# Causal scores as 64x64 tiles in a linear-attention and expert kernel, with their evacuation split over two engines

## The chip, the cores and the metric

The kernel runs on one core of one Trainium2 chip. The metric is the device time of one execution in microseconds (us). A core has a matrix engine (TensorE, PE; its weight loads are shown as PEld), VectorE (DVE), ScalarE (ACT), GpSimd (POOL) and SyncE (SP), which issues most transfers. Each engine works through its own instructions in order; semaphores order the engines among each other.

## The reference, cut to what matters

Two parts follow each other. The first is a linear attention with a decay for each channel; the second a router that sends each token to two of eight experts.

```python
# q, k, v, f_logit: (B, H, S, D) = (4, 8, 768, 48), float32
f = 1.0 / (1.0 + np.exp(-f_logit))
for t in range(S):
    state = f[:, :, t, :, None] * state + np.einsum('bhd,bhe->bhde', k[:, :, t], v[:, :, t])
    y[:, :, t] = np.einsum('bhd,bhde->bhe', q[:, :, t], state)
x = y.transpose(0, 2, 1, 3).reshape(B * S, H * D)            # (3072, 384)
noisy = x @ w_gate + np.log1p(np.exp(x @ w_noise)) * noise    # (3072, 8)
# the two largest of each row, softmax over them; for expert e of its tokens:
out[mask] += weight * (np.maximum(x[mask] @ w1[e], 0) @ w2[e])   # w1 384x1024, w2 1024x384
```

## The kernel before

**Attention.** The sequence is cut into 6 chunks of C = 128 tokens; with 4 batches this gives 24 blocks, n = 0 to 23, chunk n // 4 of batch n % 4. The 8 heads lie in 4 pairs (hp); the two heads of a pair (par) take 64 partitions each, 48 channels padded to 64. For one block the stages are:

- `forget(n)`: PE turns f over (fp, L533), ACT takes exp and ln (L538, L539) and copies the first column to a cap (L542).
- `summed(n)`: DVE's scan along the tokens gives the summed log decay L (L547).
- `decays(n)`: ACT makes P = exp(-L) and Q = exp(L) (L552, L554) and keeps the last column (far, L555).
- `scaled(n)`: PE turns q and k over (qp, kp, L533); DVE multiplies them out of PSUM by P and Q: qP (L559), kQ (L561).
- `scores(n)`: PE turns kQ back (kp, L567; ACT copies it to kn, L569), then eight products of 64 rows by 128 columns give the scores sc of 128 keys by 128 queries for each head (L573), into two banks of PSUM; DVE multiplies all of it by the causal mask into A (L576).
- `output(n)`: y is the sum of two products in two banks: v with A (L591), and from the second chunk on the state with qP (L602); between them the state's growth ds (L597). ACT copies both halves of y (yT, L606) and ds (dss, L611); POOL makes the new state.
- `features(n)`: PE puts y into token rows and gives the router's logits (xp, L626); DVE sums the logits (lg, L629), ACT copies the rows (xs, L631), SP stores them.

**Order.** The order of the program is the order of tracing, fixed on every engine at the end. Step i of the loop traces, one after the other, `forget(i+3)`, `scaled(i+1)`, `scores(i)`, `summed(i+2)`, `output(i-1)`, `decays(i+2)`, `features(i-2)`. After each stage comes a piece of the router of a finished chunk, among them three small ACT functions (sp, L646 to L648), one more (ex, L663), small DVE operations, and two small products on PE (rk, L690, L691). The single-bank tiles of PSUM (`one_bank`) come from six buffers; a new tile waits for the last reader of the buffer that has come free. The tile sc has a pool of its own with two banks.

**Head.** SP loads the first blocks. DVE writes `ones` and the padding; warming products of `ones` with itself (L1233) keep PE busy, six at first and four after each of the steps i = -3, -2 and -1. `clamp(n)` bounds f from below, on DVE for blocks 0 and 1, on POOL after that (L527). Between clamp 3 and clamp 4 POOL writes the fixed part of the router's table w_rt (L1241, L1244) and `carry` (L1246, L1247); the rest of w_rt comes by eight small transfers from POOL's queue (L496).

**Experts.** From about 150 us on PE runs the products of the eight experts (L907, L932, L1014), with gathers and scattered additions through POOL's queue. The first pieces of it stand among the last attention steps.

Of the kernel before, what the change touches and what calls it, by code (L numbers as in the profile page):

```python
# [10 lines left out]
F32 = mybir.dt.float32  # L11
# [5 lines left out]
ALU = mybir.AluOpType  # L17
# [314 lines left out]
def kernel(  # L332
# [38 lines left out]
    nc = tc.nc  # L371
    B, H, S, D = q.shape
# [3 lines left out]
    C = 128  # L376
    NCH = S // C
    HP = H // 2
    DP = 64
# [37 lines left out]
    wk = attention.enter_context(tc.tile_pool(name="wk", bufs=2))  # L417
    ps2 = attention.enter_context(tc.tile_pool(name="ps2", bufs=1, space=PSUM))
    turns = [ps1]

    def one_bank(name):
        turns.append(turns.pop(0))
        return turns[-1].tile([128, 512], F32, tag="one", name=name)

    def two_banks(name):
        return ps2.tile([128, 2, 512], F32, tag="two", name=name)


    ident = const.tile([128, 128], F32, tag="ident", name="ident")
# [36 lines left out]
    causal = const.tile([128, 128], F32, tag="causal", name="causal")  # L466
# [20 lines left out]
    w_rt = const.tile([128, HP, XW + 2 * E], F32, tag="w_rt", name="w_rt")  # L487
# [14 lines left out]
    carry = const.tile([128, E, B + 1], F32, tag="carry", name="carry")  # L502
    upto = [None] * NCH
    far = const.tile([128, NCH * B, HP], F32, tag="far", name="far")
    state = [None] * B
# [6 lines left out]
    def rows(par):  # L512
        return slice(par * DP, (par + 1) * DP)

    def cols(hp):
        return slice(hp * C, (hp + 1) * C)
# [46 lines left out]
    def scores(n):  # L563
        if n // B < NCH - 1:
            kp = one_bank(f"kp_{n}")
            for hp in range(HP):
                nc.tensor.transpose(kp[:, cols(hp)], kQ[n][:, cols(hp)], ident)  # L567
            kn[n] = wk.tile([C, H, DP], F32, tag="kn", name=f"kn_{n}")
            nc.scalar.copy(kn[n].rearrange("t h d -> t (h d)"), kp)  # L569
        sc = two_banks(f"sc_{n}")  # L570
        for hp in range(HP):
            for par in range(2):
                nc.tensor.matmul(sc[:, par, cols(hp)], lhsT=kQ[n][rows(par), cols(hp)],  # L573
                                 rhs=qP[n][rows(par), cols(hp)], start=True, stop=True)
        A[n] = wk.tile([C, 2, HP * C], F32, tag="A", name=f"A_{n}")
        nc.vector.tensor_tensor(A[n].rearrange("j r (a i) -> j (r a) i", i=C), sc.rearrange("j r (a i) -> j (r a) i", i=C),  # L576
                                causal.unsqueeze(1).broadcast_to((C, H, C)), ALU.mult)

    def output(n):
        c, b = n // B, n % B  # L580
        vt = pads["v"][n % RING["v"]]


        y = [one_bank(f"y{odd}_{n}") for odd in range(2)]

        def at(hp, par):
            return y[hp % 2][rows(par ^ hp % 2), cols(hp // 2)]

        for hp in range(HP):
            for par in range(2):  # L590
                nc.tensor.matmul(at(hp, par), lhsT=vt[:, 2 * hp + par, :], rhs=A[n][:, par, cols(hp)],  # L591
                                 start=(hp < 2), stop=(c == 0 and hp >= HP - 2))
        if c < NCH - 1:
            ds = one_bank(f"ds_{n}")
            for hp in range(HP):
                for par in range(2):
                    nc.tensor.matmul(ds[rows(par), hp * DP:(hp + 1) * DP], lhsT=kn[n][:, 2 * hp + par, :],  # L597
                                     rhs=vt[:, 2 * hp + par, :], start=True, stop=True)
        if c:
            for hp in range(HP):  # L600
                for par in range(2):
                    nc.tensor.matmul(at(hp, par), lhsT=state[b][rows(par), hp, :],  # L602
                                     rhs=qP[n][rows(par), cols(hp)], start=False, stop=(hp >= HP - 2))
        yT[n] = wk.tile([128, 2, HP // 2 * C], F32, tag="yT", name=f"yT_{n}")
        for odd in range(2):
            nc.scalar.copy(yT[n][:, odd, :], y[odd][:, 0:HP // 2 * C])  # L606
        if c == NCH - 1:
            return

        dsv = wk.tile([128, HP, DP], F32, tag="ds", name=f"dss_{n}")  # L610
        nc.scalar.copy(dsv, ds[:, 0:HP * DP].rearrange("d (a e) -> d a e", e=DP))  # L611
        end = P[n].rearrange("d (a t) -> d a t", t=C)[:, :, C - 1:C].broadcast_to((128, HP, DP))
        new = wk.tile([128, HP, DP], F32, tag=f"st{b}", name=f"st_{n}")
        if c == 0:
            nc.gpsimd.tensor_tensor(new, dsv, end, ALU.mult)
        else:
            mid = wk.tile([128, HP, DP], F32, tag="mid", name=f"mid_{n}")
            nc.gpsimd.tensor_tensor(mid, dsv, state[b], ALU.add)
            nc.gpsimd.tensor_tensor(new, mid, end, ALU.mult)
        state[b] = new  # L620
# [617 lines left out]
    pad("v")  # L1238
    clamp(2)
    clamp(3)  # L1240
    nc.gpsimd.memset(w_rt, 0.0)  # L1241
    for odd in range(2):
        for r in range(2):
            nc.gpsimd.tensor_copy(w_rt[:, odd::2, r * D:(r + 1) * D],  # L1244
                                  ident[:, (r ^ odd) * DP:(r ^ odd) * DP + D].unsqueeze(1).broadcast_to((128, HP // 2, D)))
    nc.gpsimd.memset(carry, 1.0)  # L1246
    nc.gpsimd.memset(carry[:, :, 0:1], 0.0)  # L1247

    def zeros(count):
        for _ in range(count):  # L1250
# [7 lines left out]
    def first_loads():  # L1258
# [4 lines left out]
        for what, p, pause in (("fetch", 1, 4), ("first", 0, 0), ("second", 0, 3), ("fetch", 2, 5), ("first", 1, 1), ("second", 1, 6),  # L1263
# [13 lines left out]
            for _ in range(pause):  # L1277
                yield

    def tables():  # L1280
        for i, val in enumerate((0, 0, FAR, 0)):
            nc.gpsimd.memset(empty[:, :, i], val)
        nc.gpsimd.memset(entry, 0)
        for i, ids in ((0, row_of), (2, token)):
            nc.gpsimd.tensor_copy(entry[:, :, :, :, i], ids.unsqueeze(3).broadcast_to((128, NCH, B, 2)))
        nc.gpsimd.memset(zero, 0.0)
# [5 lines left out]
    for i in range(-3, NS + 2):  # L1292
        order = [(forget, -3), (scaled, -1), (scores, 0), (summed, -2), (output, 1), (decays, -2), (features, 2)]
        if i < 0:
            order[0:2] = order[1::-1]
        for stage, lag in order:
            n = i - lag
            if not 0 <= n < NS:
                continue
            stage(n)  # L1300
            if stage is forget:
                load("f", n + 4)
                if n > 1:
                    clamp(n + 2)
                if n == 5:
                    tables()
            elif stage is scaled:
                for nm in "qk":
                    load(nm, n + 2) if n < 4 else load(nm, n + 3)
                    if n == 3:  # L1310
                        load(nm, n + 3)
                if n in (1, 2):
                    load_router(n - 1)
            elif stage is scores:
                for m in (n + 1,) if n < 4 else (2 * n - 3, 2 * n - 2) if n < 6 else (n + 3,):
                    load("v", m)
                if n in (2, 6, 7, 8, 9, 10):
                    load_router(2 + (2, 6, 7, 8, 9, 10).index(n))
                elif n == 5:
                    nc.sync.dma_start(out=lists.rearrange("(p r) w -> p r w", p=128), in_=empty)  # L1320
            elif stage is output:
                while xw:
                    xw.pop(0)()
                if 9 <= n < 17:
                    part_of_weights(0, 1 + (n - 9) // 4, (n - 9) % 4)
                elif n >= NS - 2:
                    part_of_weights(1, 1, 1 + (n - NS + 2) * 2)
            elif stage is features and n >= NS - 4:
                part_of_weights(1, 1, (n - NS + 4) * 2) if n < NS - 2 else zeros(4)
            next(router, None)  # L1330
            slot += 1
            if puts and slot % (2 if n_routed == HALF else 3) == 0 and not (done["fetch"] and not done["gather"]):
                puts.pop(0)()
            next(first_pairs, None)

            if done["turned"] and (n_first < 5 or i >= NS - 3 and stage is not forget) and (n_first < 11 or i >= NS - 1):
                next(pieces)
                n_first += 1
        if i < 0:
            warm_up(4)  # L1340
        if i >= NS - 1:
            while xw:
                xw.pop(0)()
        n = i - 2
        if n >= 0 and n % B == B - 1:
            c = n // B
            router = chain(router, route(c))
            n_routed = c + 1
            if c == HALF - 1:
                router = chain(router, enough())  # L1350
                first_pairs = first_loads()
            if c == NCH - 1:
                router = chain(router, plan(), beyond())
# [79 lines left out]
```

## Time and profile before

| what | value |
|---|---|
| median of 3 runs | 652.21 us (651.7 to 653.2) |
| the profiled execution | 652.09 us, span 650.3 us |
| PE busy | 634.9 us, 98% of the span |
| DVE, POOL, ACT busy | 443.4, 270.4, 253.9 us |
| attention steps with a state product, xp to xp | 6.00 us (88.71 to 94.71), 6.4 to 6.6 where the router's product falls in |
| scores sc (L573), 16 passes | 1.09 us of PE in a step |
| first fp on PE | 4.03 us |
| last xp on PE | 151.83 us |

The span runs from the first to the last instruction of the program. In the lines of the profile "x16" counts instructions, and each float32 product that isn't a transposition shows as two. In a timeline line the first number is the start, the second the time from the first start to the last end, and in brackets stands the idle time just before it and what ended it.

### The profile page before, as it was taken

The numbers are of one execution on the slowest core, as the hardware profiler recorded it, in microseconds if no ns is written. First come the engines' busy times: TensorE is split into PE (matmuls) and PEld (weight loads), VectorE is DVE, ScalarE is ACT, GpSimd is POOL, SyncE is SP. The second block draws the span as 40 slices with busy tenths as digits, with TensorE's granted clock in tenths as the row PEclk, the third lists the DMA queues.
The fourth block names the chain that finished last, engine by engine and source line by source line (L and its number), as shares of the span: only waits on it lengthen the run. The fifth ranks groups of instructions, "written<-read, shape, count | busy, mean of one in ns | idle before, by whom it ended". The sixth has DMA issues, their size and how long they took to land.

```text
span 650.3 us, 12900 instructions
## 1 busy us (share of the span) xinstructions
PE 634.9 (98%) x4883; PEld 549.6 (85%) x4883; DVE 443.4 (68%) x993; ACT 253.9 (39%) x602; POOL 270.4 (42%) x301
## 2 busy tenths in 40 slices
PE   8999999999999999999999999999999999999991
PEld 8999999989999999989659956985797589899891
DVE  6777878875766477776757666666666566867851
ACT  6976776752222233343333233223323322333320
POOL 7733999863474540532603350343145014413021
PEclk9999999999999999999999999999999999999997
DMA  9999888969896332459609361844376057502112
GB/s 186 194 229 209 182 192 173 205 173 341 256 214 172 74 74 98 96 135 308 195 1 305 46 191 40 281 99 120 105 217 156 33 178 168 172 3 30 17 26 29
DMA packets 153896, 96.30 MB, mean 148 GB/s; under 512 B 115600, under 2 KB 146320, under 8 KB 153824
## 3 DMA queue, kind: packets, MB, share of 16 engines
q1 hardware_dynamic: 141648, 76.12, 42.6%
q0 software_dynamic: 12176, 19.25, 15.1%
q8 instruction: 41, 0.67, 0.4%
q14 instruction: 31, 0.25, 0.1%
HBM read 75.97 MB, written 19.62 MB: 147 GB/s over the span
## 4 chain that ended last, share of the span: by engine, by line
PE 95%; POOL 1%; DMA 1%; SPq 0%; DVE 0%; issue 0%; POOLq 0%
PE y L1014 33%; PE P L932 8%; PE hp L907 6%; PE W L932 5%; PE Z L932 5%; PE V L932 5%; PE X L932 5%; PE xp L626 4%; PE sc L573 4%; PE y L591 4%; PE xgp L855 2%; PE y L602 2%; PE kp L533 2%; PE qp L533 1%; PE ds L597 1%; PE fp L533 1%
## 5 line engine op out<-in xcount | busy, mean ns | idle before, releaser
L1023 POOL DMA_INDIRECT out_dram<-ys,slots x48 | 80.8, 1683 | 162.2 <-ACT ys L1084 132.9
L1014 PE MATMUL y<-qk_all,f_all 128*128 128x192 f32 x576 | 105.3, 327 | 0.0
L1014 PEld LDWEIGHTS y<-qk_all,f_all 128*128 128x128 f32 x576 | 93.3, 190 | 0.4 <-DVE f_all L996 0.4
L819 POOL DMA_INDIRECT xg<-x_rows,slots x48 | 52.6, 1095 | 30.8 <-DMA slots<-lists 15.5
L703 POOL DMA_INDIRECT lists<-entry,sloti x48 | 54.8, 1142 | 10.3 <-issue 9.1
L1014 PE MATMUL y<-w,hs_b 128*128 128x192 f32 x320 | 59.1, 328 | 0.0
L1014 PEld LDWEIGHTS y<-w,hs_b 128*128 128x128 f32 x320 | 52.9, 190 | 0.9
L1158 POOL DMA_INDIRECT out_dram<-ys_q,slots_q x5 | 8.6, 1710 | 104.7 <-DVE ys_q L1156 104.7
L968 ACT ACTIVATE hs_b<-hs_b 128x256 f32<-128x256 f32 (+1 forms) x32 | 15.1, 471 | 71.4 <-DVE hs_b L948 71.4
L907 PE MATMUL hp<-xt_a,w 128*128 128x256 f32 x192 | 42.4, 380 | 0.0
L907 PEld LDWEIGHTS hp<-xt_a,w 128*128 128x128 f32 x192 | 36.2, 190 | 4.7
L932 PE MATMUL X<-xt_a,w 128*128 128x256 f32 (+1 forms) x128 | 39.7, 432 | 0.0
L932 PE MATMUL Z<-xt_b,v_all 128*128 128x256 f32 (+1 forms) x128 | 39.7, 432 | 0.0
L1073 DVE TENSOR_TENSOR ys<-P,y 128x192 f32<-128x192 f32 x24 | 8.5, 354 | 43.1 <-PE y L1014 27.7
L948 DVE TENSOR_TENSOR hs_b<-hs_a,X 128x256 f32<-128x256 f32 (+1 forms) x32 | 15.6, 487 | 30.6 <-PE X L932 30.1
L1084 ACT ACTIVATE ys<-ys,slots 128x384 f32<-128x384 f32 x23 | 14.1, 615 | 55.9 <-DVE ys L1080 54.0
L1014 PE MATMUL y<-w,f_all 128*128 128x192 f32 x192 | 35.2, 327 | 0.0
L576 DVE TENSOR_TENSOR A<-sc,causal 128x1024 f32<-128x1024 f32 x24 | 29.3, 1220 | 7.7 <-PE sc L573 7.6
L932 PEld LDWEIGHTS Z<-xt_b,v_all 128*128 128x128 f32 x128 | 24.3, 190 | 10.1
L932 PEld LDWEIGHTS X<-xt_a,w 128*128 128x128 f32 x128 | 24.3, 190 | 10.1
L948 DVE TENSOR_TENSOR hs_a<-hs_a,P 128x256 f32<-128x256 f32 (+1 forms) x64 | 31.1, 486 | 1.4
L1014 PEld LDWEIGHTS y<-w,f_all 128*128 128x128 f32 x192 | 31.8, 190 | 0.0
(200 smaller groups left out, 1438.5 us busy)
## 6 DMA issues: line engine op xcount, KB each, us to landing
w<-in_moe_w_dram SPq DMA_DIRECT2D x16, 1536.0 KB, 7.6
w_q<-in_moe_w_dram SPq DMA_DIRECT2D x10, 1536.0 KB, 10.2
w<-in_moe_w_dram SPq DMA_DIRECT2D x16, 384.0 KB, 5.7
f_all<-in_f_logit_dram SPq DMA_DIRECT2D x24, 192.0 KB, 3.1
qk_all<-in_q_dram SPq DMA_DIRECT2D x24, 192.0 KB, 4.2
qk_all<-in_k_dram SPq DMA_DIRECT2D x24, 192.0 KB, 4.0
v_all<-in_v_dram SPq DMA_DIRECT2D x24, 192.0 KB, 4.3
x_rows<-xs SPq DMA_DIRECT2D x24, 192.0 KB, 3.8
```

Of the source, the lines that this page charges most:

```text
L533: nc.tensor.transpose(p[:, cols(hp)], flat[:, cols(hp)], ident)
L573: nc.tensor.matmul(sc[:, par, cols(hp)], lhsT=kQ[n][rows(par), cols(hp)], rhs=qP[n][rows(par), cols(hp)], start=True, stop=True)
L576: nc.vector.tensor_tensor(A[n].rearrange("j r (a i) -> j (r a) i", i=C), sc.rearrange("j r (a i) -> j (r a) i", i=C), causal.unsqueeze(1). ...
L591: nc.tensor.matmul(at(hp, par), lhsT=vt[:, 2 * hp + par, :], rhs=A[n][:, par, cols(hp)], start=(hp < 2), stop=(c == 0 and hp >= HP - 2))
L626: nc.tensor.matmul(xp[:, hp, :], lhsT=yT[n][:, hp % 2, cols(hp // 2)], rhs=w_rt[:, hp, :], start=True, stop=True)
L703: into = nc.gpsimd.indirect_dma_start(out=lists, out_offset=bass.IndirectOffsetOnAxis(ap=sloti[:, r, b:b + 1], axis=0), in_=entry[:, c, b, ...
L819: nc.gpsimd.indirect_dma_start(out=xg[p][:, s, :], out_offset=None, in_=x_rows[0:HALF * B * C] if p < NE else x_rows, in_offset=bass.Indir ...
L907: nc.tensor.matmul(hp[:, o, :], lhsT=w1[home(k)][:, i, (fo + o) * 128:(fo + o + 1) * 128], rhs=xt_a[:, i, k % 2 * 256:(k % 2 + 1) * 256], ...
L932: nc.tensor.matmul(to, lhsT=x, rhs=y, start=start, stop=stop)
L948: nc.vector.tensor_tensor(to, x, y, ALU.add)
L1014: nc.tensor.matmul(P[name], lhsT=x[:, o, :], rhs=y[:, o, :], start=(o == 0), stop=(o == FH - 1))
L1023: into = nc.gpsimd.indirect_dma_start(out=out, out_offset=bass.IndirectOffsetOnAxis(ap=slots[p][:, s, 2:3], axis=0), in_=ys[s], in_offset= ...
```

## The change

- The scores of a block lie in one tile `sc_all` of the same two banks for the whole attention, cleared once. Only what is not above the diagonal is computed, in halves of T = 64 keys: the early keys against all 128 queries, the late keys against the late 64. For pairs 0 and 1 the early keys go to partitions 0 to 63 and the late ones to 64 to 127; for pairs 2 and 3 (heads 4 to 7) it is the other way round.
- A is one tile `A_all` with two places, whose quarter of late keys by early queries is cleared once for pairs 2 and 3. It is filled by one DVE product with the mask for pairs 0 and 1, and for pairs 2 and 3, crossing partitions, by an ACT copy (early keys, late queries) and two DVE products of 64 partitions.
- The state product of the block before moves from the end of `output` to `scores`, ahead of the scores, in a function `from_state`.
- v stays whole: the product of v with A keeps all 128 keys as its depth.
- Warming products after step -2 alone; `router_tables` is traced on POOL after clamp 4.

```diff
+    T = C // 2
+    sc_all = ps2.tile([128, 2, HP, C], F32, tag="two", name="sc_all")
+    nc.vector.memset(sc_all, 0.0)
+    A_all = wk.tile([C, 2, 2, HP, C], F32, tag="A_all", name="A_all", bufs=1)
+    nc.vector.memset(A_all[T:, :, :, HP // 2:, 0:T], 0.0)
...
-        sc = two_banks(f"sc_{n}")
-        for hp in range(HP):
-            for par in range(2):
-                nc.tensor.matmul(sc[:, par, cols(hp)], lhsT=kQ[n][rows(par), cols(hp)],
-                                 rhs=qP[n][rows(par), cols(hp)], start=True, stop=True)
-        A[n] = wk.tile([C, 2, HP * C], F32, tag="A", name=f"A_{n}")
-        nc.vector.tensor_tensor(A[n].rearrange("j r (a i) -> j (r a) i", i=C), sc.rearrange("j r (a i) -> j (r a) i", i=C),
-                                causal.unsqueeze(1).broadcast_to((C, H, C)), ALU.mult)
+        if n:
+            from_state(n - 1)
+        for hp in (0, 2, 1, 3):
+            for late_rows in range(2):
+                half = hp // 2 ^ late_rows
+                for par in range(2):
+                    nc.tensor.matmul(sc_all[half * T:(half + 1) * T, par, hp, late_rows * T:],
+                                     lhsT=kQ[n][rows(par), hp * C + late_rows * T:hp * C + (late_rows + 1) * T],
+                                     rhs=qP[n][rows(par), hp * C + late_rows * T:(hp + 1) * C], start=True, stop=True)
+        A[n] = A_all[:, n % 2]
+        near, far_ = slice(0, HP // 2), slice(HP // 2, HP)
+        low, high = slice(0, T), slice(T, C)
+
+        def masked(to, whole_, at):
+            nc.vector.tensor_tensor(to, whole_, at.unsqueeze(1).unsqueeze(1).broadcast_to(whole_.shape), ALU.mult)
+
+        masked(A[n][:, :, near, :], sc_all[:, :, near, :], causal)
+        nc.scalar.copy(A[n][low, :, far_, high], sc_all[high, :, far_, high])
+        masked(A[n][low, :, far_, low], sc_all[high, :, far_, low], causal[high, high])
+        masked(A[n][high, :, far_, high], sc_all[low, :, far_, high], causal[low, low])
+
+    def place(n, hp, par):
+        return y_of[n][hp % 2][rows(par ^ hp % 2), cols(hp // 2)]
+
+    def from_state(n):
+        y_of[n] = [one_bank(f"y{odd}_{n}") for odd in range(2)]
+        if n // B:
+            for hp in range(HP):
+                for par in range(2):
+                    nc.tensor.matmul(place(n, hp, par), lhsT=state[n % B][rows(par), hp, :],
+                                     rhs=qP[n][rows(par), cols(hp)], start=(hp < 2), stop=False)
...
-        if c:
-            for hp in range(HP):
-                for par in range(2):
-                    nc.tensor.matmul(at(hp, par), lhsT=state[b][rows(par), hp, :],
-                                     rhs=qP[n][rows(par), cols(hp)], start=False, stop=(hp >= HP - 2))
...
-    nc.gpsimd.memset(w_rt, 0.0)
-    for odd in range(2):
-        for r in range(2):
-            nc.gpsimd.tensor_copy(w_rt[:, odd::2, r * D:(r + 1) * D],
-                                  ident[:, (r ^ odd) * DP:(r ^ odd) * DP + D].unsqueeze(1).broadcast_to((128, HP // 2, D)))
-    nc.gpsimd.memset(carry, 1.0)
-    nc.gpsimd.memset(carry[:, :, 0:1], 0.0)
...
+    def router_tables():          # the same seven operations
...
-                if n == 5:
-                    tables()
+                if n in (2, 5):
+                    (router_tables if n == 2 else tables)()
...
-        if i < 0:
+        if i == -2:
             warm_up(4)
```

More of the change, by code (lines that the diff above doesn't have):

```diff
@@ L423, in one_bank @@
         return turns[-1].tile([128, 512], F32, tag="one", name=name)
-    def two_banks(name):
-        return ps2.tile([128, 2, 512], F32, tag="two", name=name)
+    T = C // 2
[3 more added lines that the diff above has]
+    nc.vector.memset(A_all[T:, :, :, HP // 2:, 0:T], 0.0)
     ident = const.tile([128, 128], F32, tag="ident", name="ident")
@@ L569, in scores @@
             nc.scalar.copy(kn[n].rearrange("t h d -> t (h d)"), kp)
-        sc = two_banks(f"sc_{n}")
-        for hp in range(HP):
-            for par in range(2):
-                nc.tensor.matmul(sc[:, par, cols(hp)], lhsT=kQ[n][rows(par), cols(hp)],
-                                 rhs=qP[n][rows(par), cols(hp)], start=True, stop=True)
-        A[n] = wk.tile([C, 2, HP * C], F32, tag="A", name=f"A_{n}")
-        nc.vector.tensor_tensor(A[n].rearrange("j r (a i) -> j (r a) i", i=C), sc.rearrange("j r (a i) -> j (r a) i", i=C),
-                                causal.unsqueeze(1).broadcast_to((C, H, C)), ALU.mult)
+        if n:
[16 more added lines that the diff above has]
+        masked(A[n][high, :, far_, high], sc_all[low, :, far_, high], causal[low, low])
+    y_of = {}
+    def place(n, hp, par):
[7 more added lines that the diff above has]
+                                     rhs=qP[n][rows(par), cols(hp)], start=(hp < 2), stop=False)
     def output(n):
@@ L581, in output @@
         vt = pads["v"][n % RING["v"]]
-        y = [one_bank(f"y{odd}_{n}") for odd in range(2)]
-        def at(hp, par):
-            return y[hp % 2][rows(par ^ hp % 2), cols(hp // 2)]
+        if n not in y_of:
+            from_state(n)
+        y = y_of[n]
         for hp in range(HP):
             for par in range(2):
-                nc.tensor.matmul(at(hp, par), lhsT=vt[:, 2 * hp + par, :], rhs=A[n][:, par, cols(hp)],
-                                 start=(hp < 2), stop=(c == 0 and hp >= HP - 2))
+                nc.tensor.matmul(place(n, hp, par), lhsT=vt[:, 2 * hp + par, :], rhs=A[n][:, par, hp, :],
+                                 start=(c == 0 and hp < 2), stop=(hp >= HP - 2))
         if c < NCH - 1:
@@ L1278, in first_loads @@
                 yield
+    def router_tables():
+        nc.gpsimd.memset(w_rt, 0.0)
+        for odd in range(2):
+            for r in range(2):
+                nc.gpsimd.tensor_copy(w_rt[:, odd::2, r * D:(r + 1) * D],
+                                      ident[:, (r ^ odd) * DP:(r ^ odd) * DP + D].unsqueeze(1).broadcast_to((128, HP // 2, D)))
+        nc.gpsimd.memset(carry, 1.0)
+        nc.gpsimd.memset(carry[:, :, 0:1], 0.0)
     def tables():
```

## The prediction

> **What bounds the kernel now.** I read the page first, then the chain of waits in order of time, then the timeline of ScalarE (ACT) and VectorE (DVE) over a few steps of the attention loop.
>
> ```profile
> PE 634.9 (98%) x4883; PEld 549.6 (85%) x4883; DVE 443.4 (68%) x993; ACT 253.9 (39%) x602; POOL 270.4 (42%) x301
> PE 95%; POOL 1%; DMA 1%; SPq 0%; DVE 0%; issue 0%; POOLq 0%
> ...
> 85.60 1.09 PE sc L573 x16
> 86.70 1.02 PE y L591 x16
> 87.72 0.47 PE ds L597 x16
> 88.18 0.60 PE y L602 x16
> 88.78 1.07 PE xp L626 x8
> 89.86 0.44 PE fp L533 x4
> ```
>
> The chain of waits is TensorE (PE) for 95%. A step of the attention loop (first to about 150 us) takes it 6.00 us, fp to fp (83.86 to 89.86); four of the steps carry a router product of 0.4 to 0.6 us more. A saving on PE shortens a step only if no other ring of work is as long, so I looked at what the two evacuating engines do in one step:
>
> ```profile
> 40.66 0.65 ACT L552 ACTIVATE P<-L 128x512 f32<-128x512 f32 x1
> 41.19 0.64 ACT L554 ACTIVATE Q<-L 128x512 f32<-128x512 f32 x1
> 41.71 0.20 ACT L555 COPY far<-L 128x4 f32<-128x4 f32 x1
> 41.80 0.49 ACT L631 COPY xs<-xp 128x384 f32<-128x384 f32 x1
> 42.17 0.62 ACT L538 ACTIVATE f<-fp 128x512 f32<-128x512 f32 x1
> 42.83 0.63 ACT L539 ACTIVATE f<-f 128x512 f32<-128x512 f32 x1
> 43.49 0.20 ACT L542 COPY cap<-f 128x4 f32<-128x4 f32 x1
> 43.59 0.23 ACT L646 ACTIVATE sp<-lg 128x32 f32<-128x32 f32 x1
> 44.24 0.57 ACT L569 COPY kn<-kp 128x512 f32<-128x512 f32 x1
> 45.86 0.65 ACT L606 COPY yT<-y 128x256 f32<-128x256 f32 x2 [1.04 <-PE y L602]
> ...
> 48.49 0.68 DVE L561 TENSOR_TENSOR kQ<-kp,Q 128x512 f32<-128x512 f32 x1
> 49.79 1.23 DVE L576 TENSOR_TENSOR A<-sc,causal 128x1024 f32<-128x1024 f32 x1 [0.27 <-PE sc L573]
> 50.93 1.22 DVE L547 TENSOR_TENSOR_SCAN L<-f,cap 128x512 f32<-128x512 f32 x1
> ```
>
> The reader is to see start-to-start times: P to kn 2.93 us without sp (0.65 more with it), A to the scan 1.14, and that both engines idle for PE once a step. The scan releases P 1.245 after its start (14.67 to 15.92 in the first steps). So a closed ring runs beside PE: A, scan, P, qP, kQ, A = 1.14 + 1.245 + 0.66 + 0.61 + 0.60 = 4.25 us, which is how far apart P(2) and P(3) stand (15.92 and 20.16), before PE takes over.
>
> **The change part by part.** *Scores on PE.* The matmul records of one step show two passes per product; in sc a pair of row tiles starts every 0.106 us, in L602 four 64x64 tiles every 0.109. Each of four quarters now gets 128+64+128+64 columns in two passes: 4 x 0.109 + 4 x 0.058 (the ds interval for 64 columns) = 0.67 us. L602 moves ahead of sc and has the same 64x64 shape, so one change of shape goes. From the last kp transposition to the first xp, before: 0.20 + 1.09 + 0.92 + 0.56 + 0.60 = 3.38; after: 0.20 + 0.49 + 0.67 + 0.09 + 0.92 + 0.56 = 2.94. PE saves 0.44 in each of 20 steps, 0.28 in the first four, which have no L602: 9.9 us if PE stays the bound, and a step of 5.56.
>
> *Evacuating the scores.* DVE's 1024-wide product becomes a 512-wide one, an ACT copy and two 64-partition products of 256. In the changed program's order the copy waits for the first product, the second for the copy, and the scan stands behind the third. Costs: 0.69 (as L559, 512 from PSUM) + 0.04; copy 0.37 (the 128x256 yT row) + 0.04; two products of 0.34 each, issue to issue (1.14 at 1024 and 0.61 at 512 give 1.04 ns an element and 0.08 fixed). Sum 1.82 where 1.14 stood: +0.68. Nothing shows a 64-partition form; bounds are 1.5 and 2.1. Behind the waiting copy are queued yT, yT, dss, P, Q, xs; behind the waiting products the scan, so P.
>
> [...] The row: the product on sc is followed at once by the scan, and DVE has idled only 0.27 to 0.61 us for PE in these steps. [...]
>
> *The rings after.* (A) ACT's own: copy to P = 0.41 + 0.34 + 0.34 + 1.245 = 2.335; P to the next copy 2.91 + 0.52 = 3.42 (3.05 without xs). 5.76 us, and 0.65 more in a step with sp. (B) Through PE: the state product now stands before sc, and its second y bank is the one that qP(i+1) or xs of the step before has just freed (the waits of the built order; 5 and 10 steps). From start of sc: 0.88 to its evacuation, 0.73 to the copy, 2.335 to P; then P to end of qP and PE 1.435, or to end of xs and PE 1.70; then 0.40 to the next sc. 5.78 by qP, 6.05 by xs. All are longer than PE's 5.56, and about the old 6.00.
>
> *Stage by stage* (P(n) by its start). Head: DVE clears the score banks (128x1024) and part of A (64x512) ahead of `ones`, for which all PE work waits. The nearest row is POOL's memset of 128x512, 0.515: 1.5 us for both (0.9 to 2.0). The first fp comes 1.5 later; fp 1 no longer stands behind four warming matmuls (4.91 to 6.47), which gives back about 0.5: +1.0 (0.4 to 1.5). First chunk: copy 0 waits behind kn, so P(2) is 1.1 later still; P(2) to P(6) is 2 x 5.39 + 2 x 5.76 = 22.3 where the trace has 18.9: +3.4. So P(6) is at 34.84 + 5.5 = 40.4, the state product at 41.8, sc 5 at 42.2, xp 3 2.25 later at 44.5 instead of 39.76: +4.7. Steps 5 to 18, xp 3 to xp 17: before 85.7; after 10 x 6.05 + 4 x 5.78 = 83.6, + sp in four of them 2.2, + router work between A and the scan 0.95 (45.48 - 44.93 once, 0.4 once), + ex ahead of xs 4 x 0.11: 87.2, +1.5. Last steps: PE saves 4 x 0.44, the longer evacuation takes 0.68 in the two that DVE paces (A at 130.42, 135.56, 139.87): -0.4. After that PE runs the experts without a gap, so all of it is carried: 4.7 + 1.5 - 0.4 = +5.8.
>
> *Hidden edits.* Warming matmuls: 16 passes of 0.11 to 0.21 us leave PE where it waits for POOL or ACT[...]. Router tables: 2.5 us of POOL (10.02 to 12.57) go behind clamp 4, which then waits for its DMA (issued 8.71, 3.4 to land: 12.1), so it gains 0.4, behind a PE that waits for ACT anyway. Moved past: clamp 4 alone; clamp 5 and the eight table DMAs behind come up to 2.2 later, their last landing at 23.1 + 2.2 = 25.3, when xp 0 is due (25.2); if PE were early it would cost up to 2 us. SP's queue keeps its order.
>
> The sum stands against the profiled execution: 652.09 (span 650.3 and 1.8 around it), 0.1 under the median of the runs, 652.21. 652.1 + 5.8 = 657.9.
>
> **The rivals.** *PE stays the bound* (faster): a step of 5.56, 9.9 saved, 1.0 lost in the head: 643. For it: PE is 98% busy and ACT and DVE are not. It decides from the point where xs or qP frees the y bank 0.5 us earlier than I have it, that is where evacuation and scan follow sc by 1.33 instead of 1.82. Against: the copy alone, between two semaphores, is 0.41. 0.08. *The rings are 0.25 shorter*: 652, the early loss just paid back by 20 steps. 0.17: half of it within 0.2%, a quarter on either side. *The quarters do not overlap* (scores on PE stay near 1.09, and in ring B they are on the path): 15 steps by up to 0.4 more, 663. 0.08. *The change does not do what it says*: no; the built order shows 16 products a step of 64x128 and 64x64.
>
> **How the numbers follow.** My forecast, +2 to +10, has 0.67: 657.9. A measurement of this kernel can tell about 0.2%, 1.3 us. Low end: memsets 0.9 (-0.6), rings 0.1 shorter in 18 steps (-1.8), sp and router work hidden (-3), last steps -1.8 instead of -0.4: 651. High end, quarters overlapping by half: 663. Faster 0.08 + 0.05 = 0.13; same 0.08; slower 0.67 + 0.08 + 0.04 = 0.79.
>
> **What would show it.** Right: in the first chunk the P rows about 5.8 us apart instead of 5.4; from step 5 the period near 6.0 although sc takes 0.7 to 0.8 instead of 1.09; PE idle ahead of the state product, released by DVE qP or ACT xs, some 0.3 to 0.5 us a step; the ACT copy waiting for DVE and DVE for the copy; PE busy under 98%; the first fp near 5.5. Wrong: a period of 5.6 with no wait ahead of the state product (rival one), or a copy that does not hold the second product.

## The result, and the profile after

The changed kernel takes 674.8 us (median of 4 runs, 672.91 to 675.5) against 651.96 in the runs beside it: 1.0342 of the kernel before, 95% interval 1.0317 to 1.0367, so 22.8 us slower. The forecast was 657.9 with a range of 651 to 663: the right side, and a quarter of the size. The profiled execution took 674.82 us (span 673.0).

Its page, the row of engines and the chain of waits:

```profile
PE 635.6 (94%) x5251; PEld 549.7 (82%) x5251; DVE 455.3 (68%) x1043; ACT 265.3 (39%) x626; POOL 279.4 (42%) x301
PE 79%; DVE 10%; ACT 7%; issue 2%; POOL 0%; POOLq 0%; DVEq 0%; ACTq 0%
```

PE's busy time is nearly the same as before (635.6 after, 634.9 before) in a span 22.7 us longer: it now waits. In the chain PE holds 79% instead of 95%, and DVE and ACT 17% where they had next to nothing. From the last xp to the end of the span both kernels take the same (498.5 before, 498.3 after), so all of the loss lies ahead of the last xp, which came at 151.8 and comes at 174.7.

The chain of waits in order of time, one step of the changed kernel in which no router work falls on the chain:

```profile
101.17 0.49 ACT xs L652
...
101.70 0.55 PE y L604 x10
...
102.32 0.77 PE sc_all L579 x15
...
103.11 0.70 DVE A_all L587
...
103.83 0.38 ACT A_all L590
...
104.24 0.43 DVE A_all L587
...
104.68 0.42 DVE A_all L587
...
105.11 1.24 DVE L L550
```

Before, this view was PE from row to row. Now it walks over three engines: xs frees the y bank, the state product and the scores follow, then first product, copy, second and third product, scan. The scores take 0.77 us in this step instead of 1.09, and none of that comes out at the end. The views of waits of PE, ACT and DVE up to 175 us (sum, times, longest) say the same:

```profile
PE y L604 <- ACT xs L652: 7.2, 6, 2.1
PE y L604 <- DVE qP L562: 4.0, 3, 2.2
...
ACT P L555 <- DVE L L550: 19.6, 16, 2.2
ACT xs L652 <- DVE lg L650: 8.5, 10, 1.2
...
DVE A_all L587 <- ACT A_all L590: 16.6, 24, 1.4
```

DVE waits for the copy in all 24 blocks. The row `ACT xs <- DVE lg` was not in my sum: xs needs lg, so whatever DVE does ahead of lg holds xs, and with it the y bank and PE. The timeline of DVE, ACT and PE in a step with router work:

```profile
84.41 0.66 DVE L672 SCALAR_TENSOR_TENSOR sp<-lg,sp 128x32 f32<-128x32 f32 x1
...
85.32 0.50 DVE L674 TENSOR_TENSOR nz<-sp,lg 128x32 f32<-128x32 f32 x1
...
86.55 0.20 DVE L650 TENSOR_REDUCE lg<-xp 128x16 f32<-128x64 f32 x1
...
86.79 0.48 ACT L652 COPY xs<-xp 128x384 f32<-128x384 f32 x1 [0.97 <-DVE lg L650]
...
87.32 0.55 PE L604 MATMUL y<-qP,st 64*64 64x128 f32 x10 [1.82 <-ACT xs L652]
```

The router's pieces fill DVE from 84.41 to 86.55, lg comes after them, xs after lg, and the state product, four of whose instructions had run at 85.07, stands still for 1.82 us. What then follows is in the table by stretches (length, busy time of PE, PEld, DVE, ACT, POOL, then the granted clock, the DMA share and GB/s), the first two rows of the changed kernel, the third of the kernel before:

```profile
80.00:86.00 6.00, 5.50 (x96) 4.96 (x88) 4.30 (x9) 4.40 (x13) 5.02 (x8) 1.00 0.81 190
86.00:92.00 6.00, 4.68 (x80) 4.49 (x80) 5.32 (x22) 3.98 (x10) 3.57 (x6) 0.73 0.78 174
...
86.00:92.00 6.00, 6.00 (x94) 5.47 (x92) 3.51 (x6) 4.25 (x12) 5.43 (x9) 1.00 0.69 125
```

The granted clock falls to 0.50 for 3.41 us (88.76 to 92.17). That happens three times (from 58.04, 88.76 and 116.06 us), each after a PE wait of 1.8 to 2.2 us, and never in the trace of before between the first 7 us and the end of the work (granted clock 1.00 from 7 to 640 us). Not every such wait is followed by it; see the end.

### The profile page after: what moved, and what is told of

Its sections match the earlier page's. It is cut to its first block, busy times and chain, and to the rows that moved or that the text cites. A ratio compares the mean times of both kernels' runs of the same rounds, so it can differ in the third digit from the quotient of the medians.

```text
span 673.0 us, 13691 instructions
## 1 busy us (share of the span) xinstructions
PE 635.6 (94%) x5251; PEld 549.7 (82%) x5251; DVE 455.3 (68%) x1043; ACT 265.3 (39%) x626; POOL 279.4 (42%) x301
## 3 DMA queue, kind: packets, MB, share of 16 engines
q0 software_dynamic: 12176, 19.25, 14.7%
## 4 chain that ended last, share of the span: by engine, by line
PE 79%; DVE 10%; ACT 7%; issue 2%; POOL 0%; POOLq 0%; DVEq 0%; ACTq 0%
PE y L1035 32%; PE P L953 8%; PE hp L928 6%; PE W L953 5%; PE V L953 5%; PE X L953 5%; PE Z L953 5%; DVE L L550 3%; DVE A_all L587 3%; PE xgp L876 2%; PE sc_all L579 1%; ACT f L542 1%; PE xp L647 1%; PE yp_q L1173 1%; PE y L604 1%
## 5 line engine op out<-in xcount | busy, mean ns | idle before, releaser
L1035 PE MATMUL y<-qk_all,f_all 128*128 128x192 f32 x576 | 105.3, 327 | 0.0
L587 DVE TENSOR_TENSOR A_all<-sc_all,causal 64x256 f32<-64x256 f32 (+1 forms) x72 | 36.7, 510 | 28.0 <-ACT A_all L590 16.6
L724 POOL DMA_INDIRECT lists<-entry,sloti x48 | 51.2, 1066 | 10.7 <-issue 9.2
L639 POOL TENSOR_TENSOR mid<-dss,st 128x256 f32<-128x256 f32 x16 | 19.8, 1235 | 33.0 <-ACT dss L632 33.0
L953 PEld LDWEIGHTS X<-xt_a,w 128*128 128x128 f32 x128 | 24.3, 190 | 10.1
L953 PEld LDWEIGHTS Z<-xt_b,v_all 128*128 128x128 f32 x128 | 24.3, 190 | 10.1
## 6 DMA issues: line engine op xcount, KB each, us to landing
w_q<-in_moe_w_dram SPq DMA_DIRECT2D x10, 1536.0 KB, 10.3
```

The lines of the kernel that those rows point to most:

```text
L587: nc.vector.tensor_tensor(to, whole_, at.unsqueeze(1).unsqueeze(1).broadcast_to(whole_.shape), ALU.mult)
L724: into = nc.gpsimd.indirect_dma_start(out=lists, out_offset=bass.IndirectOffsetOnAxis(ap=sloti[:, r, b:b + 1], axis=0), in_=entry[:, c, b, ...
L953: nc.tensor.matmul(to, lhsT=x, rhs=y, start=start, stop=stop)
L1035: nc.tensor.matmul(P[name], lhsT=x[:, o, :], rhs=y[:, o, :], start=(o == 0), stop=(o == FH - 1))
```

## The experiments

They ran later, on four chips (the column *chip* has the number on record; for the first pair none is), on each of which the kernel before takes 665 to 667 us instead of 652. Every ratio below is to runs of the kernel before on the same chip. Two traces of unchanged kernels place the difference. *xp 3* and *last* are the first rows of xp 3 and of the last xp, *stretch* is xp 3 to xp 17, all in us of one profile. One profile says little about a few us of the stretch: before, before_again and e_head_only, whose instructions are the same there, have 85.7, 88.7 and 91.7.

| kernel | chip | ratio, 95% interval | P(2) to P(6) | xp 3 | stretch | last |
|---|---|---|---|---|---|---|
| before, first runs |  | | 18.9 | 39.8 | 85.7 | 151.8 |
| after, first runs |  | 1.0342 (1.0317 to 1.0367) | 23.9 | 46.5 | 101.1 | 174.7 |
| before_again | 11 | one run | 19.4 | 40.2 | 88.7 | 167.7 |
| after_again | 11 | 1.0351 (1.0309 to 1.0393) | 23.8 | 46.2 | 105.3 | 189.2 |
| e_split_only | 11 | 1.0282 (1.0225 to 1.0338) | 24.9 | 45.0 | 99.5 | 184.2 |
| e_state_back | 2 | 1.0288 (1.0239 to 1.0336) | 23.8 | 45.6 | 98.6 | 184.4 |
| e_state_ahead_only | 2 | 1.0106 (1.0032 to 1.0179) | 19.4 | 40.2 | 97.0 | 175.1 |
| e_one_product | 11 | not compared | 19.8 | 41.3 | 92.0 | |
| e_router_held | 9 | one run, not compared | 23.9 | 46.5 | 86.3 | |
| e_copy_last | 9 | 1.0107 (1.0069 to 1.0145) | 19.2 | 40.9 | 97.0 | 176.7 |
| e_copy_last_back | 8 | 1.0026 (1.0010 to 1.0042) | 19.2 | 40.9 | 86.4 | 165.9 |
| e_late_clear | 8 | 1.0001 (0.9987 to 1.0015) | 19.2 | 39.9 | 86.1 | 164.0 |
| e_head_only | 2 | 1.0007 (0.9984 to 1.0029) | 19.3 | 41.3 | 91.7 | 169.8 |
| e_straight | 2 | 1.0042 (1.0017 to 1.0067) | 19.9 | 40.6 | 88.0 | 168.6 |
| e_v_swapped | 9 | 1.0281 (1.0253 to 1.0309) | 20.9 | 42.9 | 100.7 | 184.6 |

**before_again and after_again.** No edit.

> The kernel before, unchanged, for its trace on the chip that these runs share: if the chip's own pace makes the difference to the 652 us of before, its lost time lies in waits that no edit has touched (DMA of k and q, instruction issue around 145 to 165 us), and the steps of 6.0 us are there wherever those waits are not.

> The changed kernel, unchanged, on the chip that these runs share: 1.02 to 1.035 of before, first chunk P(2) to P(6) 23.9 us, xp 3 to xp 17 near 101 us with steps of 7 to 10 where the router works.

The loss is the same share in these runs. Their own 13 to 15 us more lie mostly behind xp 17: of the 15.8 us between the two profiles of the kernel before, 3.0 are in the stretch and 12.5 between xp 17 and the last xp. PE's waits from 120 to 180 us and one stretch of before_again:

```profile
PE y L591 <- issue: 2.4, 4, 1.3
PE sc L573 <- issue: 2.0, 5, 0.6
```

```profile
146.00:154.00 8.00, 5.37 (x29) 3.22 (x28) 0.00 (x0) 0.37 (x1) 6.51 (x12) 0.71 0.56 126
```

PE stops after every few products for nothing that the profile shows, ACT and DVE stand nearly still, and the clock falls. The cause is open: the expectations put it down to the chip, but four chips have it, and on which the first pair ran is not on record. All kernels of these runs with the router in its place show it (xp 17 to the last xp takes 26.4 us in the first trace of before, 36.9 to 41.0 in these); e_router_held has no such stop before its last xp. So the columns up to xp 17 are the better measure of an edit.

**e_split_only: is the split enough?**

```diff
-        nc.vector.tensor_tensor(A[n]..., sc..., causal..., ALU.mult)
+        masked(A[n][:, :, near, :], sc[:, :, near, :], causal)
+        nc.scalar.copy(A[n][low, :, far_, high], sc[low, :, far_, high])
+        masked(A[n][low, :, far_, low], sc[low, :, far_, low], causal[low, low])
+        masked(A[n][high, :, far_, high], sc[high, :, far_, high], causal[high, high])
```

> The kernel before, scores in full tiles and the state product in its old place, with only the evacuation split as in the change: a 512-wide product, a ScalarE copy of one quarter and two products of 64 partitions (here without a change of partitions; the cleared quarter of A is never written). Theory (the split evacuation alone makes the loss): P(2) to P(6) 23 to 24.5 us, xp 3 to xp 17 over 95, 1.02 to 1.035 of before. Rival (it takes the moved state product as well): 1.005 to 1.012, the early loss alone, and steps near 6.1 after it. A smaller loss in the early steps than in the changed kernel would say that crossing partitions has a price of its own.

Nearly: 1.0282 by the split alone, where the whole change has 1.0351. Its timeline (DVE, then ACT):

```profile
30.73 0.68 DVE L584 TENSOR_TENSOR A_all<-sc,causal 128x512 f32<-128x512 f32 x1
32.64 0.88 DVE L584 TENSOR_TENSOR A_all<-sc,causal 64x256 f32<-64x256 f32 x2 [1.23 <-ACT A_all L587]
33.55 1.65 DVE L550 TENSOR_TENSOR_SCAN L<-f,cap 128x512 f32<-128x512 f32 x1
...
32.25 0.36 ACT L587 COPY A_all<-sc 64x256 f32<-64x256 f32 x1
```

The copy stands behind kn on ACT and starts at 32.25; DVE, done with the first product at 31.41, idles 1.23 us for it. Nothing here crosses partitions, and the copy and the pair of products take the same as in the changed kernel (0.36 and 0.88 us here, 0.37 and 0.88 there), so the crossing has no price that shows. (P(2) to P(6) is even 1.0 us longer, because the scans take 1.65 us there instead of 1.23; see the end.)

**e_state_back and e_state_ahead_only: the state product's place.**

```diff
 # e_state_back: in scores(n)
-        if n:
-            from_state(n - 1)
 # in output(n), behind ds; v with A opens the banks again
+        from_state(n)
```

> The changed kernel with the state product put back behind ds, everything else as changed. Theory (most of the loss in steps 5 to 18 is the state product in its new place, waiting for a y bank that xs or qP frees late): the first chunk stays (P(2) to P(6) near 23.9 us), then steps of about 6.15 without router work, no wait of over 1 us on TensorE, no stretch at half clock, and a time of 658 to 664 us. Rival (the evacuation in four instructions alone sets the steps, wherever the state product stands): 670 to 676 us, with steps of 7 to 9 us where the router works.

> The kernel before with only the state product moved ahead of the scores; scores and the single VectorE product as before. Theory of the two together (the place hurts through ring B, and ring B is shorter with one product in place of four instructions: about 5.7 us): steps without router work stay at 6.0, those with router work gain 0.5 to 2 us; 654 to 662 us. Rival (the place alone costs all of it): 668 or more, with the half-clock stretches. Rival (the place is free without the split evacuation): 650.5 to 653.

My theory fell in the first: 1.0288, most of the loss stays with the state product in its old place, the stretch falls only from 105.3 to 98.6, and PE waits of 1.4 to 2.3 us are left there, one of them followed by half clock. In the second the place alone costs 1.0106, which was within what I expected of the two together. Its waits were few (four for xs, 4.1 us up to 140 us), but two of them, 3.1 us between 96 and 120 us, were followed by 6.8 us at half clock (granted clock 0.54 from 111 to 118 us).

**e_one_product: quarters without the split.**

```diff
-        (four instructions)
+        nc.vector.tensor_tensor(A[n]..., sc_all..., causal..., ALU.mult)
```

> The changed kernel with one 1024-wide VectorE product on the score tile in place of the two kinds of products and the copy: heads 4 to 7 are not put back in place, so y of these heads is computed from misplaced keys. TensorE's work, its order, the head and the tables are as changed. Theory (the four-instruction evacuation sets the steps): P(2) to P(6) falls to 17.5 to 20 us, xp 3 to xp 17 to 80 to 88, no half-clock stretch; 0.985 to 1.005 of before. Rival (the state product's place costs it): xp 3 to xp 17 stays over 95, 1.015 or more.

P(2) to P(6) comes back to 19.8, as expected; the stretch to 92.0 rather than the 80 to 88 of the theory, with one wait-and-half-clock event again (steps of 8.3 and 10.1). Beside after_again, on the same chip, that is 13 us less, which go with the split and with the longer half clock there (granted clock 0.97 from 46.2 to 151.4 us). The 3.3 us left beside before_again are too few to be told from the scatter of single profiles. The time as a whole (976.8 us) isn't read: keys are misplaced, and what follows the last xp takes 802 us instead of 498.

**e_router_held: what does the bare ring take?**

```diff
-            next(router, None)
+            if i >= NS - 4:
+                next(router, None)
```

> The changed kernel with the router's pieces held back until xp 17 (they run later, so the total is longer and is not compared); only the stretch xp 3 to xp 17 is read. Theory (a closed ring of 6.15 us, and all router work on VectorE and ScalarE comes on top of it): 14 steps of 6.0 to 6.2, 84 to 88 us in all, no half-clock stretch; the 101 to 105 us of the changed kernel is then 15 to 18 us of router work and what follows from it. Rival (waits for y banks or a slow clock without the router's help): over 93.

14 steps in 86.33 us, 6.17 each, no half clock. The chain, one turn of the ring:

```profile
79.97 0.70 DVE qP L562
...
80.72 0.55 PE y L604 x10
...
81.33 0.77 PE sc_all L579 x15
...
82.12 0.70 DVE A_all L587
82.84 0.38 ACT A_all L590
...
83.25 0.44 DVE A_all L587
83.70 0.43 DVE A_all L587
84.15 1.24 DVE L L550
...
85.47 0.64 ACT P L555
...
86.14 0.70 DVE qP L562
```

This is a closed ring through all three engines, qP to qP in 6.17 us. The same stretch by engine (busy PE, PEld, DVE, ACT, POOL), of this kernel, of the changed kernel and of the kernel before:

```profile
46.46:132.79 86.33, 83.96 (x1461) 76.33 (x1457) 58.29 (x99) 65.99 (x169) 46.63 (x41) 1.00 0.88 196
```

```profile
46.47:147.52 101.05, 90.34 (x1474) 82.64 (x1471) 77.66 (x202) 70.37 (x185) 70.03 (x89) 0.95 0.76 164
```

```profile
39.76:125.46 85.70, 85.70 (x1251) 78.22 (x1247) 68.64 (x174) 62.94 (x170) 65.20 (x86) 1.00 0.91 198
```

The router puts 19.4 us more on DVE and 4.4 on ACT, and the stretch is 14.7 us longer (18.9 beside after_again). In the kernel before, the third row, the 14 steps took 85.7 us, only 1.7 more than 14 times the 6.00 of a step without router work: PE was busy throughout, and the pieces cost it no wait. With every engine a link of one ring, most of them have no place to hide. PE's 6.4 us more hold the router's own products and the half-clock time.

**e_copy_last: the same four instructions in another order.**

```diff
-        nc.scalar.copy(A[n][low, :, far_, high], sc_all[high, :, far_, high])
         masked(A[n][low, :, far_, low], ...)
         masked(A[n][high, :, far_, high], ...)
+        nc.scalar.copy(A[n][low, :, far_, high], sc_all[high, :, far_, high])
```

> The changed kernel with the ScalarE copy issued behind the two 64-partition products instead of between the first and the second product: the same four instructions, but VectorE no longer waits for ScalarE in the middle. Theory (the loss is the ring copy, two products, scan, P, and back over ScalarE's stream to the next copy, because VectorE waits for the copy): from the first product to the scan 1.6 us instead of 2.0, the ring is cut to about 5.0 us, P(2) to P(6) 19.5 to 22, xp 3 to xp 17 between 86 and 96 on this chip, 1.003 to 1.018 of before. Rival (the added VectorE time as such, with the router's work on top): P(2) to P(6) stays over 23 and the ratio over 1.025.

The changed kernel's timeline of DVE in a step without router work, then that of e_copy_last (DVE, then ACT):

```profile
45.13 0.69 DVE L587 TENSOR_TENSOR A_all<-sc_all,causal 128x512 f32<-128x512 f32 x1 [0.86 <-PE sc_all L579]
46.26 0.88 DVE L587 TENSOR_TENSOR A_all<-sc_all,causal 64x256 f32<-64x256 f32 x2 [0.44 <-ACT A_all L590]
47.16 1.23 DVE L550 TENSOR_TENSOR_SCAN L<-f,cap 128x512 f32<-128x512 f32 x1
```

```profile
28.96 1.59 DVE L587 TENSOR_TENSOR A_all<-sc_all,causal 128x512 f32<-128x512 f32 x3
30.58 1.23 DVE L550 TENSOR_TENSOR_SCAN L<-f,cap 128x512 f32<-128x512 f32 x1
...
30.64 0.37 ACT L592 COPY A_all<-sc_all 64x256 f32<-64x256 f32 x1
...
31.90 0.63 ACT L555 ACTIVATE P<-L 128x512 f32<-128x512 f32 x1
```

First product to scan: 1.62 us instead of 2.03, and P(2) to P(6) falls from 23.8 to 19.2, although 0.4 us a step is all that was taken out of the sequence. The ring is what was cut: while DVE waited for the copy and the copy for ACT's whole stream, both streams were strung into one line. The ratio falls from 1.0351 to 1.0107. P(2) to P(6) is just below and the stretch, 97.0, just above what I expected, with a half-clock event (a step of 10.3).

**e_copy_last_back and e_late_clear: the rest, and a better version.**

```diff
 # e_late_clear: e_copy_last, the state product behind ds, the head of the kernel before, and
     pad("v")
+    nc.vector.memset(sc_all[T:, :, 0:HP // 2, 0:T], 0.0)
+    nc.vector.memset(A_all[T:, :, :, HP // 2:, 0:T], 0.0)
```

> The changed kernel with the ScalarE copy last and the state product back behind ds; head and tables as changed. Theory (the state product's place is what is left of the loss in steps 5 to 18, since it brings the y bank's wait 0.7 us forward): xp 3 to xp 17 falls from 97.0 to 86 to 91 us, 0.998 to 1.005 of before. Rival (VectorE's longer evacuation still sets the steps in which the router works): over 93, 1.008 or more.

> The version that may beat both: scores in quarters, evacuation with the copy last, state product in its old place, and the head of the kernel before (warming matmuls and router's table as before, the two clearing memsets behind the pads and only as large as needed). Theory: P(0) at 8.2 to 8.6 us and 1.0 us less than with the changed head; steps without router work 5.6 to 5.9 instead of 6.0; 0.990 to 1.000 of before. Rival (no gain is left, since VectorE's four instructions take what TensorE saves): 1.000 to 1.008.

With both undone (e_copy_last_back) the stretch is 86.4, and steps without router work take 5.7 us instead of 6.0: now the cheaper scores show. Part of the chain of e_late_clear:

```profile
53.83 0.44 PE kp L568 x4
54.27 0.82 PE sc_all L575 x24
55.08 1.04 PE y L610 x16
```

The scores take 0.82 us for 1.09, and PE binds again. Still the whole is only level with before: 1.0001, which lies on the border of theory and rival and decides for neither. In the profiles its last xp is 3.7 us earlier than that of before_again, but the timed runs show no gain; whether one would be seen without the stops behind xp 17 was not tried. It has the lowest ratio of the versions with quarters. It differs from e_copy_last_back in the head alone and ran on the same chip, so the two price the head: 664.45 us (22 runs) against 665.66 (20 runs), 1.2 us.

**e_head_only, e_straight, e_v_swapped.** The first is the kernel before with the changed head. The second keeps the quarters on the partitions of their keys, the third exchanges the halves of v's rows for heads 4 to 7 as they are loaded (kn and the mask follow); both keep one product of 1024:

```diff
 # e_v_swapped: load of v, three transfers in place of one
+            for to, at, heads in ((slice(0, C), slice(0, C), slice(0, H // 2)), (low, high, slice(H // 2, H)), (high, low, slice(H // 2, H))):
+                nc.sync.dma_start(out=pads["v"][...][to, heads, 0:D], in_=whole_v[at, heads, :])
```

> The kernel before with only the head of the change: the two clearing memsets on VectorE ahead of ones, fewer warming matmuls, the router's table later. Theory: 1.0 us, all carried to the end, 653 us. Rival: the later table or the missing warming matmuls cost a wait or a slow clock of their own, 655 or more. Rival: hidden, 652.

> The kernel before with causal scores whose quarters stay on the partitions of their keys (early keys on 0 to 63 for all queries, late keys on 64 to 127 for late queries), so that the single VectorE product is kept; the late-by-early quarter is cleared once, behind the pads; state product, warming and tables as before. If TensorE binds before and the four-instruction evacuation is what made the change slow: sc takes 0.85 to 0.95 instead of 1.09, some 0.15 to 0.25 saved in each of 20 steps, 647 to 650 us. Rival (the rings of ScalarE and VectorE are already as long as TensorE's step): 651.5 to 653. Rival (quarters of unequal width do not overlap, sc 1.1 or more): 652 to 654.

> A version that keeps the four 64x64 tiles of the scores and drops the putting back in place: for heads 4 to 7 the halves of v's rows are exchanged as they are loaded (three DMAs in place of one), kn is turned with exchanged halves on TensorE (four 64-column products for the two far pairs), the mask tile has the exchanged quarter, and one 1024-wide VectorE product evacuates the scores. State product, warming matmuls and tables as before. If the split evacuation was all that stood against the cheaper scores: sc 0.65 to 0.75, steps of 5.5 to 5.7, xp 3 to xp 17 at 80 to 85 on this chip (88.7 before), 0.985 to 0.993 of before. Rival (SP's queue, with two more DMAs a step, holds back k and q): 0.995 to 1.01. Rival (the rings of VectorE and ScalarE with the router's work are as long as TensorE's step already): 0.997 to 1.003.

e_head_only: P(0) and xp 3 are 1.2 and 1.1 us later than in before_again, as forecast; in the timed runs that is not to be told from nothing (1.0007, interval 0.9984 to 1.0029), inconclusive for the total. e_straight: its scores take 1.02 us (73.50 to 74.52). In it the early keys of all four pairs go to partitions 0 to 63, 4 x 128 queries, where the exchanged order (0.77 to 0.82 us) has 384 on either half; whether this is the reason was not shown. No saving, and 1.0042; why it is even a little slower is open. e_v_swapped: its theory fell, and of its rivals the one of SP's queue fits, at a larger size than I gave it (1.01 at most). Waits of ACT (40 to 145 us) and of PE (up to 145 us):

```profile
ACT xs L647 <- DMA x_rows<-xs: 21.5, 11, 3.8
...
PE kp L543 <- DMA qk_all<-in_k_dram: 5.2, 4, 1.8
```

In before_again the first of these waits is 3.5 us in all and the second does not occur. With two more transfers a step in one queue, of the same bytes, the stores of xs and the loads of k come late; the whole costs 2.8%, as much as the split. The turned kn was not run apart from the transfers.

## Why the prediction was right or wrong

The sum had three terms, the head being part of the first; in the two traces of the first runs they measure:

| term | forecast | measured |
|---|---|---|
| head: P(0) | +1.0 | +1.1 |
| xp 3, head included | +4.7 | +6.7 |
| xp 3 to xp 17 | +1.5 | +15.4 |
| xp 17 to last xp | -0.4 | +0.8 |
| sum | +5.8 | +22.9 |

- *What bounds, and the rings*: right in kind. PE's saving did not reach the end; ring A, named and walked in the prediction, set the first chunk, and the ring through PE the steps after it. Rival one (643) and the rival of shorter rings are refuted by the chain; the quarters do overlap (0.71 to 0.82 us, forecast 0.67). That it came out slower for the reasons given was not luck; the size was missed further down.
- *Head*: right (first fp at 5.67, forecast 5.5).
- *First chunk, mis-sized by 2.0*: the 64-partition products, for which the trace of before had no row, take 0.45 from issue to issue and not 0.34, the scan releases P 1.32 after its start instead of 1.245, P to the next copy is 3.51 for 3.42. Together 0.4 a step: 6.14 where I had 5.76. That makes 1.55 from P(2) to P(6); the other 0.45 came before P(2). The split is 2.03 us from first product to scan, inside my bounds of 1.5 to 2.1, at their upper end.
- *Ring through PE, mis-sized*: 5.78 to 6.05 forecast, 6.17 without router work; 86.3 for the stretch instead of 83.6, that is +2.7. From sc to the copy I was right (1.51 measured, 1.61 forecast); copy to P is 2.63 instead of 2.335, and from qP's arrival to the next sc 0.62 instead of 0.40. I had xs free the y bank last in ten of the 14 steps (6.05); with the router held it is qP in all 14.
- *Router work, the step that failed*: I charged 2.2 for sp (four times my own 0.65 would be 2.6), 0.95 for DVE pieces between A and the scan, and 0.44 for ex: 3.6 us. The traces with and without the router differ by 14.7 us (101.05 and 86.33), and 9.9 of it lies in three steps, of 9.8, 9.0 and 9.7 us, in which the router's small pieces stand ahead of qP or of lg. I had looked for router work only on the stretch of DVE between A and the scan. But once the ring passes through all of DVE's stations, a piece anywhere between the scan and qP beyond the 0.64 us that DVE idles there lengthens it, and so does one ahead of lg, which holds xs and thereby the state product. The prediction named qP and xs as releasers and did not ask what stands ahead of them.
- *Half clock, left out*: in the same three steps, 3 x 3.41 us at half speed, at most 5.1 us of those 14.7 if PE worked through all of it. How the 14.7 divide between it and the ring is not shown.
- *Last steps*: 0.8 lost where I had 0.4 gained; no run looks at them alone.

Which part of the change carries the loss is shown: the copy in the middle of the evacuation (1.0351 to 1.0107 by moving that one line), then the state product's place (1.0107 to 1.0026), then the head (1.0026 to 1.0001). Alone, the split costs 2.8% and the place 1.1%. The use of two engines is one thing, the wait between them another: with the same two engines and the same four instructions, the kernel takes 2.4% longer (1.0351 against 1.0107) when one has to wait for the other halfway.

## What to carry to other kernels

When work is split over two in-order engines, add up not the instructions but the ring that the wait between them closes (6.17 us here): everything queued ahead of each waiting instruction is in it, and so is every odd job that had filled a gap before (14.7 us of the stretch here). Issue the other engine's part last, so that the one on the path never waits for it (1.0107 instead of 1.0351 here). A product moved to an earlier place on PE brings its buffer's wait forward with it (alone 1.0106 here); look up which reader frees that buffer, and what stands ahead of that reader.

## What the hardware showed

- In the first trace of the changed kernel, PE waits of 2.21, 1.82 and 2.08 us (from 55.89, 85.50 and 113.83) were each followed by 3.41 us at a granted clock of 0.50 (from 58.04, 88.76 and 116.06). Such a wait is not enough by itself: in after_again one of 2.58 us (at 92.13) was followed by half clock, but waits of 2.22, 1.82, 1.85 and 2.03 us (at 55.59, 84.12, 124.92 and 145.51) were not. In the 3.41 us ahead of the three falls in the changed kernel PE was busy for 1.26, 1.59 and 1.33 us; from 13.65 to 17.07 us it was busy for 2.15, and the granted clock stayed at 1.00. What decides whether a fall follows was not shown.
- The same scan takes 1.23 us, or 1.64 to 1.78 when a POOL product (st or mid) had started just before it. Over all 15 traces that holds for 12 of the 13 scans with such a product already running (7 of the 12 in e_split_only, one each in the traces of before and after). Of the 112 scans during which a product started, none took over 1.27; there the product is the one that takes longer, 1.46 to 1.67 us if it starts within 0.3 us of the scan, against 0.62 to 0.74 where it came first. A POOL bound running at the start went with a longer scan in only 5 of 46 cases (1.33 to 1.56). Small DVE pieces go from 0.17 to 0.66 as well beside a POOL product (sp, L672 of the changed kernel: 0.66 at 84.41 with mid running, 0.17 at 142.24 without a product).
- In the later runs PE stops without a visible cause for some 0.2 to 1.3 us after every few products around 146 to 157 us of before_again, an unchanged kernel; the first trace of before has no such stop.
